# Folding two pieces of an expert's first weights at a time, over four PSUM banks

## Chip, cores and metric

The kernel runs on one core of a Trainium2 chip. The metric is the device time of one execution in microseconds (us).

## What is computed

Three stages in float32: attention through 32 packed tokens a head, four experts whose outputs are weighted, and a two-layer MLP. The sizes: batch 4, 8 heads, 576 tokens, head size 64 (2304 rows of 512 in all); the experts go from 512 to 1024 and back, the last layer from 512 to 2048 and back.

```
p_packed = sm_attn(p, k, v)               # 32 rows a head
x = sm_attn(q, p_packed, p_packed)        # reshaped to 2304 x 512
for e in range(4):
    h = max(x @ w1[e], 0)
    out += p[:, e:e+1] * (h @ w2[e])
g = s * max(out @ w_in, 0)**2 + b
y = g @ w_out
```

## The kernel before

Every product is done in three matmuls of float32r halves (low x high, high x high, high x low); a tile called `hi` is the rounded value and `lo` the rest.

The attention's last product and the experts' first are joined: instead of `(a @ p_packed) @ w1` the kernel multiplies `p_packed @ w1` first, once for each batch, and calls that the fold. Its result `w1p` (128 packed rows of a head group by 512 columns, hi and lo) is then the stationary operand of `m1` (line 726), which makes `h`; ScalarE and VectorE evict `h` as `hh` and `hl` (lines 747 and 749), and `m2` (line 772) adds their products with `w2` into `acc`.

The experts run through 256 steps: expert `e`, batch `bi`, half `hf` of the tokens, block `f` of 128 columns, 16 steps a batch. `m1` runs two steps ahead of `m2`. `m2` holds two or three of four PSUM banks (`acc0` to `acc3`, taken in turn); `h` has two, and the tag `m` has two.

Expert 0's folds are done in place for each batch. For experts 1 to 3 the fold is done for all batches at once, in pieces named by expert, column half `n` (columns 0 to 511 or 512 to 1023), head group `gi` and `x`:

- `load_w1b` (line 519) loads `w1r` for one (`n`, `gi`), 512 KB;
- `split_w1b` (529) makes its hi and lo for one `x`, on ScalarE and VectorE;
- `fold_heads` (541) does six matmuls into the two `m` banks: for `z` 0 and 1 in turn the upper or lower 64 rows of the array, three products each (tile `pp`, line 546), then four evictions to `w1o` (ScalarE line 552, VectorE line 553);
- `store_heads` (558) stores two `w1o` of 512 KB to `w1p_dram` (line 561, issued by SP);
- `load_w1p` (567) later loads a batch's `w1p`, four pieces of 128 KB (line 573, SP), which wait for the stores that they read.

An expert has 8 such pieces, three experts 24. `w1r` and `w1o` share seven buffers (`take` and `give`, first given, first taken) with `last_weights` (line 617), which converts the last layer's float64 weights (`wi0raw` and so on) along the way.

Work is put into a table by step (`at`); at each step what stands there is issued in the order in which it was put in, then `m1`, then `m2`. Each engine and SP's queue work strictly in that order. `load_w2` (line 590) loads one block `w2r` of 256 KB into one of five buffers, which `split_w2` (598) frees: ScalarE makes `w2h` (603), GpSimd `w2l` (606).

Of the kernel before, what the change touches and what calls it, by code (L numbers as in the profile page):

```python
# [8 lines left out]
F32 = mybir.dt.float32  # L9
F32R = mybir.dt.float32r  # L10
U32 = mybir.dt.uint32
AF = mybir.ActivationFunctionType
ALU = mybir.AluOpType
# [6 lines left out]
def attention_experts_mlp_kernel(  # L20
# [25 lines left out]
    nc = tc.nc  # L46
# [5 lines left out]
    P = 128  # L52
    G = 2
    HT = S // 2
    HF = F // 2
    NF = F // P
    KB = DM // P
# [20 lines left out]
    ps_m = stack_a.enter_context(tc.tile_pool(name="ps_m", bufs=2, space=PSUM))  # L78
# [3 lines left out]
    def f32(ap):  # L82
        return ap.bitcast(F32)
# [115 lines left out]
    def flip_p():  # L199
        t = bank("pflip")  # L200
        for i in range((B - FINE) * G):
            nc.tensor.transpose(t[:64, i * P : (i + 1) * P], p_in[:, FINE * G + i], ident)
        t = t[:64].rearrange("d (i x c) -> d i x c", x=2, c=64)
        for x in range(2):
            nc.scalar.activation(pflip[half(x)], t[:, :, x], AF.Copy)
# [3 lines left out]
    def bank(name, tag="m"):  # L209
        pool = {"m": ps_m, "h": ps_h}.get(tag, ps_acc)  # L210
        return pool.tile([P, 512], F32, tag=tag, name=name)

    def half(x):
        return slice(64 * x, 64 * x + 64)

    def at_s1(bi, h, tags="mm"):
        ps = stt["s1", bi, h] = [bank(f"s1_{bi}{h}{c}", tags[c]) for c in range(2)]
        if bi >= FINE:
            for g in range(G):
                for z in range(2):  # L220
                    for x in range(2):
                        r = 64 * g + 32 * z
                        i = (bi - FINE) * G + g
                        nc.tensor.matmul(  # L224
                            ps[x][r : r + 32, :HT],
                            lhsT=pflip[half(x), i, 32 * z : 32 * z + 32],
                            rhs=kqT["k", bi, g][half(x), z, h * HT : (h + 1) * HT],
                            start=True,
                            stop=True,
                        )  # L230
            return
        for e in range(2):
            for g in range(G):
                for c in range(2):
                    x = kqT["k", bi, g][half(c), e]
                    t = ps[c][half(g), :HT]
                    if bi == 0:
                        x = x.rearrange("a (r j) -> a r j", j=NJ)[:, :, blocks((h,))[0]]
                        t = t.rearrange("a (r j) -> a r j", r=32)
                    else:  # L240
                        x = x[:, h * HT : (h + 1) * HT]
                    nc.tensor.matmul(  # L242
                        t, lhsT=pbd[bi][half(c), g, e, :], rhs=x, start=(e == 0), stop=(e == 1)
                    )
# [39 lines left out]
    def at_a1t(bi, gi, tags="mm"):  # L284
        a1, _, _ = stt["a1", bi, gi]
        a1c = a1[:, : VC * P].rearrange("a (r c) -> a c r", c=VC)
        at = att.tile([P, VC + 1, P], F32, tag="a1t", bufs=2, name=f"a1t_{bi}{gi}")
        t = bank(f"tr_{bi}{gi}0", tags[0])
        for c in range(VC):
            nc.tensor.transpose(t[:, c * P : (c + 1) * P], a1c[:, c, :], ident)  # L290
        nc.scalar.activation(
            at[:, :VC, :].rearrange("r c a -> r (c a)"), t[:, : VC * P], AF.Copy
        )
        t = bank(f"tr_{bi}{gi}1", tags[1])
        nc.tensor.transpose(t[:VR, :P], a1[:, VC * P :], ident)
        nc.scalar.activation(at[:VR, VC, :], t[:VR, :P], AF.Copy)
        stt["a1t", bi, gi] = at
# [147 lines left out]
    def take(shape, dt, name):  # L445
        tag = free4.pop(0)
        return tag, wf.tile(shape, dt, tag=tag, bufs=1, name=name)
# [44 lines left out]
    w1s = {}  # L492
# [6 lines left out]
    pth = {}  # L499
# [38 lines left out]
        if x == 1:  # L538
            give(w1q[e, n, gi])

    def fold_heads(e, n, gi, x):
        ps = [ps_m.tile([P, 512], F32, tag="m", name=f"pp1_{e}{n}{gi}{x}{z}") for z in range(2)]
        for i, (a, w) in enumerate(((1, 0), (0, 0), (0, 1))):
            for z in range(2):
                r = slice(64 * z, 64 * z + 64)
                nc.tensor.matmul(  # L546
                    ps[z], lhsT=pth[a][r, gi, x, :], rhs=w1s[e, n, gi][w][r, x, :],
                    start=(i == 0), stop=(i == 2),
                )
        for z in range(2):  # L550
            q, t = take([P, 2, HF], F32R, f"w1o_{e}{n}{gi}{x}{z}")
            nc.scalar.activation(t[:, 0], ps[z], AF.Copy)  # L552
            nc.vector.tensor_tensor(out=t[:, 1], in0=ps[z], in1=f32(t[:, 0]), op=ALU.subtract)  # L553
            w1o[e, n, gi, x, z] = q, t

    w1o = {}

# [161 lines left out]
    hh, rest, acc, xt, x2 = {}, {}, {}, {}, {}  # L719
# [116 lines left out]
    xs, gg, o_acc, o_sb, sx, yy = {}, {}, {}, {}, {}, {}  # L836
# [157 lines left out]
    with tc.manual_schedule():  # L994
# [8 lines left out]
        for gi in range(G):  # L1003
# [3 lines left out]
            out=p_rows[:NB], in_=probs.rearrange("(j a) e -> j (a e)", a=P)  # L1007
# [123 lines left out]
        SB = 2 * NF  # L1131

        def at(step, fn, *args):
            weave.setdefault(step, []).append((fn, args))
# [5 lines left out]
        def mid(step):  # L1140
            return "mid", step
# [23 lines left out]
        for n in range(1, B):  # L1165
            s0 = (n - 1) * SB + (4 if n == 1 else 0)
# [34 lines left out]
        for e in range(E):  # L1201
            for bi in range(B):
                s0 = (e * B + bi) * SB
                ne, nb = (e, bi + 1) if bi + 1 < B else (e + 1, 0)
                if ne == E:
                    continue
                for n in range(2 if ne == 0 else 0):
                    for fn in (fold_w1, fold_hi, fold_lo):
                        step = s0 + 11 + 4 * n
                        at(mid(step) if nb == 1 and n == 0 else step, fn, nb, n)  # L1210
                for c in range(4):
                    n, gi = divmod(c, 2)
                    if ne:
                        d = c + 4 * (ne == 1 and nb == 1) if nb else ((6, 7, 13, 14) if ne > 1 else (8, 8, 12, 12))[c]
                        at(s0 + d, load_w1p, ne, nb, n, gi)
                    if bi != B - 1:
                        continue
                    for x in range(2):
                        k = 2 * c + x
                        if ne == 1:  # L1220
                            d = s0 + 2 + k
                        elif n:
                            d = s0 + 2 * k - 7
                        elif ne == 2:
                            d = s0 - SB + 8 + 2 * k
                        else:
                            d = s0 - 2 * SB + NF + 2 * k
                        if x == 0:
                            at(max(d - 4, s0) if ne == 1 else d - 4, load_w1b, ne, n, gi)
                        at(d, split_w1b, ne, n, gi, x)  # L1230
                        at(d + 1, fold_heads, ne, n, gi, x)
                        at(d + (2 if ne == 1 else 3), store_heads, ne, n, gi, x)
                if bi == B - 1:
                    for f in range(NF):
                        at(s0 + (f // 2 if f < 5 else 5 + f) if ne == 1 else s0 + 6 + f, load_w2, ne, f)
                        at(s0 + 9 + f, split_w2, ne, f)
# [17 lines left out]
        s0 = (E * B - 2) * SB  # L1254
# [142 lines left out]
```

## Time and profile before

| what | value |
|---|---|
| median of 3 runs | 1078.56 us |
| lowest and highest | 1077.34 and 1079.09 us |
| span of the profiled execution, first to last instruction | 1076.6 us |
| time of runs beyond that span (1078.56 - 1076.6) | 2.0 us |
| busy: TensorE matmuls, weight loads | 1065.9 us, 906.2 us |
| busy: VectorE, ScalarE, GpSimd | 657.2, 442.5, 181.3 us |
| TensorE's granted clock | 1.0 of full speed throughout |

The profile is of one execution, whose own time is known by its span; the 2.0 us are the difference to the runs' median. Busy time of TensorE counts matmuls whose ends are modelled and which overlap, so starts are the better measure there: the distance from one start to the next is what the engine spent. Idle time of the other engines costs nothing as long as TensorE doesn't wait for them.

### The profile page before, as it was taken

Reading aid. Unit: us, or ns where it says so; the run is one execution under the profiler, and the core shown is the slowest. Engines: PE = TensorE matmul, PEld = TensorE weight load, DVE = VectorE, ACT = ScalarE, POOL = GpSimd, SP = SyncE. Lnnn points to the kernel's source line nnn. Section 1 sums busy time; section 2 is a strip of 40 time slices with the busy share of each in tenths; the row PEclk is TensorE's granted clock in tenths of the full one; section 3 lists DMA queues with packets and bytes.
Section 4 is the critical chain, followed back from the end, with each engine's and each line's share of the span. In section 5 each row is a group of like instructions: output and inputs, shape, how many; then the busy total and the mean of one; then the engine's idle time right before and its main releaser. Section 6 shows DMA issues by size and latency. Waiting matters only on the chain.

```text
span 1076.6 us, 16978 instructions
## 1 busy us (share of the span) xinstructions
PE 1065.9 (99%) x6215; PEld 906.2 (84%) x6215; DVE 657.2 (61%) x1291; ACT 442.5 (41%) x991; POOL 181.3 (17%) x201
## 2 busy tenths in 40 slices
PE   8999999999999999999999999999999999999998
PEld 5777778788887888888888888988888888888887
DVE  7885765645365445565465645699745766775554
ACT  3533333543234343433434765766532332343111
POOL 0620312131010131010221123023101120210000
PEclk9999999999999999999999999999999999999999
DMA  9853330976555775574766242256856555665532
GB/s 267 199 108 77 50 109 19 331 217 187 143 163 213 252 188 137 187 235 161 249 171 174 68 128 118 98 193 227 330 178 216 190 200 181 209 209 183 186 108 88
DMA packets 107037, 187.01 MB, mean 174 GB/s; under 512 B 49465, under 2 KB 64057, under 8 KB 106955
## 3 DMA queue, kind: packets, MB, share of 16 engines
q1 hardware_dynamic: 106107, 184.82, 55.0%
q10 hardware_dynamic: 848, 1.11, 0.4%
q8 instruction: 49, 0.80, 0.3%
q14 instruction: 33, 0.27, 0.1%
HBM read 131.11 MB, written 54.79 MB: 173 GB/s over the span
## 4 chain that ended last, share of the span: by engine, by line
PE 93%; DVE 2%; DMA 2%; SPq 1%; issue 1%; ACT 0%; POOL 0%; DVEq 0%; ACTq 0%
PE acc L772 36%; PE h L726 19%; PE o L972 19%; PE h L936 16%; PE pp L546 2%; DMA v<-in_v_dram 1%; DMA raw<-in_moe_w_dram 1%; PE pv L308 1%; PE pw L470 0%; PE s L375 0%; PE tr L290 0%; SPq L148 0%; DVE xs L879 0%; PE s L224 0%; PE s L242 0%
## 5 line engine op out<-in xcount | busy, mean ns | idle before, releaser
L726 PEld LDWEIGHTS h<-a,w1p 128*128 128x128 f32 x1536 | 227.5, 188 | 35.5 <-issue 9.0
L726 PE MATMUL h<-a,w1p 128*128 128x320 f32 (+1 forms) x1536 | 250.7, 299 | 0.5 <-DVE hl L749 0.3
L749 DVE SCALAR_TENSOR_TENSOR hl<-h,hh 128x256 fp32r<-128x256 f32 x256 | 107.4, 420 | 203.4 <-ACT rest L747 102.2
L972 PE MATMUL o<-wo,gg 128*128 128x512 f32 x864 | 224.8, 394 | 0.0
L936 PE MATMUL h<-xs,wop 128*128 128x384 f32 x1008 | 203.8, 338 | 1.5 <-DVE yy L956 1.5
L772 PE MATMUL acc<-w2l,hh 128*128 128x512 f32 x512 | 201.9, 394 | 0.2 <-POOL w2l L606 0.2
L772 PE MATMUL acc<-w2h,hh 128*128 128x512 f32 x512 | 201.4, 393 | 0.0
L772 PE MATMUL acc<-w2h,hl 128*128 128x512 f32 x512 | 200.4, 391 | 0.0
L936 PEld LDWEIGHTS h<-xs,wop 128*128 128x128 f32 x1008 | 180.5, 188 | 16.2 <-DVE yy L956 1.8
L972 PEld LDWEIGHTS o<-wo,gg 128*128 128x128 f32 x864 | 160.2, 188 | 24.8 <-DVE gg L902 0.4
L747 ACT ACTIVATE hh<-h 128x256 fp32r<-128x256 f32 x256 | 98.3, 384 | 191.6 <-PE h L726 187.8
L772 PEld LDWEIGHTS acc<-w2h,hl 128*128 128x128 f32 x512 | 96.2, 188 | 21.9
L772 PEld LDWEIGHTS acc<-w2l,hh 128*128 128x128 f32 x512 | 96.3, 188 | 15.8 <-issue 0.4
L772 PEld LDWEIGHTS acc<-w2h,hh 128*128 128x128 f32 x512 | 96.3, 188 | 13.2
L888 ACT ACTIVATE yy<-yy 128x768 f32<-128x768 f32 x48 | 40.2, 838 | 110.0 <-DVE yy L956 110.0
L956 DVE TENSOR_TENSOR yy<-h,uv 128x384 f32<-128x384 f32 x96 | 51.0, 552 | 49.5 <-PE h L936 49.2
L898 ACT ACTIVATE gg<-yy,b_sb 128x768 fp32r<-128x768 f32 x48 | 44.8, 934 | 33.7 <-DVE yy L891 32.4
L553 DVE TENSOR_TENSOR w1o<-pp,w1o 128x512 fp32r<-128x512 f32 x48 | 30.9, 686 | 43.5 <-ACT w1o L552 43.5
L606 POOL TENSOR_TENSOR w2l<-w2r,w2h 128x512 fp32r<-128x512 f32 x24 | 31.3, 1304 | 138.5 <-ACT w2h L603 137.7
L902 DVE SCALAR_TENSOR_TENSOR gg<-yy,b_sb,gg 128x768 fp32r<-128x768 f32 x48 | 52.7, 1098 | 0.4 <-ACT gg L898 0.4
L956 DVE TENSOR_TENSOR uv<-h,uv 128x384 f32<-128x384 f32 x48 | 26.4, 554 | 38.7 <-PE h L936 38.7
L891 DVE SCALAR_TENSOR_TENSOR yy<-yy,s_sb 128x768 f32<-128x768 f32 x48 | 49.7, 1035 | 0.0
(392 smaller groups left out, 1080.7 us busy)
## 6 DMA issues: line engine op xcount, KB each, us to landing
xs<-xs_dram SPq DMA_DIRECT2D x63, 768.0 KB, 4.3
w1p_dram<-w1o SPq DMA_DIRECT2D x48, 512.0 KB, 3.7
w1p<-w1p_dram SPq DMA_DIRECT2D x192, 128.0 KB, 4.3
xs_dram<-xs SPq DMA_DIRECT2D x21, 768.0 KB, 3.3
w1r<-in_moe_w_dram SPq DMA_DIRECT2D x12, 512.0 KB, 4.3
w2r<-in_moe_w_dram SPq DMA_DIRECT2D x24, 256.0 KB, 4.3
out_dram<-o_sb SPq DMA_DIRECT2D x17, 256.0 KB, 2.0
v<-in_v_dram SPq DMA_DIRECT2D x8, 512.0 KB, 6.0
```

The lines of the kernel that those rows point to most:

```text
L606: nc.gpsimd.tensor_tensor(out=lo, in0=raw_t.pop((e, f)), in1=f32(hi), op=ALU.subtract)
L726: nc.tensor.matmul(t[:, : width(bi, hf)], lhsT=w1p_block(e, bi, f, gi, w), rhs=a2[bi][:, x, gi, part(bi, hf)], start=(n == 0), stop=(n == ...
L747: nc.scalar.activation(hi, src, AF.Relu)
L749: nc.vector.scalar_tensor_tensor(out=lo, in0=src, scalar=0.0, in1=f32(hi), op0=ALU.max, op1=ALU.subtract)
L772: nc.tensor.matmul(acc[j], lhsT=x, rhs=w, start=(f == 0 and n == 0), stop=(g == NF - 1 and n == 2),)
L888: nc.scalar.activation(y, y, AF.Relu)
L891: nc.vector.scalar_tensor_tensor(out=y, in0=y, scalar=s_sb, in1=y, op0=ALU.mult, op1=ALU.mult)
L898: nc.scalar.activation(t[:, 0], y, AF.Identity, bias=b_sb)
L902: nc.vector.scalar_tensor_tensor(out=t[:, 1], in0=y, scalar=b_sb, in1=f32(t[:, 0]), op0=ALU.add, op1=ALU.subtract)
L936: nc.tensor.matmul(ps, lhsT=w[:, a, col], rhs=x[:, z, m, :], start=(n == 0), stop=(n == 3 * HK - 1),)
L956: nc.vector.tensor_tensor(out=dst, in0=ps, in1=src, op=ALU.add)
L972: nc.tensor.matmul(o_acc[i], lhsT=lhsT, rhs=w, start=(f == 0 and n == 0), stop=(f == FG - 1 and n == 2),)
```

## The change

`fold_heads` takes a list of `x`. The first piece still goes to the two `m` banks; a second one goes to two banks of `acc` that `m2` doesn't hold at that time (`spare`). Its six matmuls follow the first piece's directly; the eight evictions follow in turn. Expert 1's first column half is folded in single pieces at the steps of before. All other pieces are folded in pairs, and the table of steps is rewritten for them: the second column half of each expert at steps 10 and 12 of its last batch ahead (before: 7 to 10 for expert 1; 2, 4, 6, 8 for experts 2 and 3), its stores at 12 and 14, its `w1p` loads for batch 0 at 13 and 15 (before: 12 and 12, or 13 and 14). The first use of them stays at step 18, two steps into the new expert.

```diff
+    def spare(i, name):
+        return bank(name, f"acc{-(acc['n'] + i) % KB}")
...
+    def fold_heads(e, n, gi, xs):
+        ps = {}
+        for x in xs:
             for z in range(2):
-                r = slice(64 * z, 64 * z + 64)
-                nc.tensor.matmul(
-                    ps[z], lhsT=pth[a][r, gi, x, :], rhs=w1s[e, n, gi][w][r, x, :],
-                    start=(i == 0), stop=(i == 2),
+                name = f"pp1_{e}{n}{gi}{x}{z}"
+                if x == xs[0]:
+                    ps[x, z] = ps_m.tile([P, 512], F32, tag="m", name=name)
+                else:
+                    ps[x, z] = spare(1 + z, name)
+        for x in xs:
+            for i, (a, w) in enumerate(((1, 0), (0, 0), (0, 1))):
+                for z in range(2):
+                    r = slice(64 * z, 64 * z + 64)
+                    nc.tensor.matmul(
+                        ps[x, z], lhsT=pth[a][r, gi, x, :], rhs=w1s[e, n, gi][w][r, x, :],
+                        start=(i == 0), stop=(i == 2),
+                    )
...
-                        d = c + 4 * (ne == 1 and nb == 1) if nb else ((6, 7, 13, 14) if ne > 1 else (8, 8, 12, 12))[c]
+                        d = c + 4 * (ne == 1 and nb == 1) if nb else ((6, 7, 13, 15) if ne > 1 else (8, 8, 13, 15))[c]
                         at(s0 + d, load_w1p, ne, nb, n, gi)
...
+                    if ne == 1 and n == 0:
+                        for x in range(2):
+                            d = s0 + 2 + 2 * c + x
+                            if x == 0:
+                                at(max(d - 4, s0), load_w1b, ne, n, gi)
+                            at(d, split_w1b, ne, n, gi, x)
+                            at(d + 1, fold_heads, ne, n, gi, (x,))
+                            at(d + 2, store_heads, ne, n, gi, x)
+                        continue
+                    d = s0 + 10 + 2 * gi if n else {
+                        2: s0 - SB + 10, 3: s0 - 2 * SB + 10
+                    }[ne] + 3 * gi
+                    at(d - 7, load_w1b, ne, n, gi)
                     for x in range(2):
...
+                        at(d - 3 + x + (n and gi), split_w1b, ne, n, gi, x)
+                        at(d + 2, store_heads, ne, n, gi, x)
+                    at(d, fold_heads, ne, n, gi, (0, 1))
```

On TensorE, the last two pieces of expert 1 (`pp1_11100` to `pp1_11111`; the digits are expert, `n`, `gi`, `x`, `z`). Before, from the end of the first piece to the start of the second:

```order
L546 MATMUL pp1_11100_2740<-w1l_111_2715,pth0_2400 128x512
L546 MATMUL pp1_11101_2741<-w1l_111_2715,pth0_2400 128x512
L726 MATMUL h_0313_2760<-a2_3_2227,w1p_0300_2252 128x256 x3
L726 MATMUL h_0313_2760<-a2_3_2227,w1p_0301_2254 128x256 x3
L772 MATMUL acc_016_2730<-w2l_01_430,hh_0311_2674 128x512
L772 MATMUL acc_016_2730<-w2h_01_429,hh_0311_2674 128x512
L772 MATMUL acc_016_2730<-w2h_01_429,hl_0311_2675 128x512
L772 MATMUL acc_017_2734<-w2l_01_430,hh_0311_2674 128x512
L772 MATMUL acc_017_2734<-w2h_01_429,hh_0311_2674 128x512
L772 MATMUL acc_017_2734<-w2h_01_429,hl_0311_2675 128x512
L546 MATMUL pp1_11110_2781<-w1h_111_2714,pth1_2401 128x512
L546 MATMUL pp1_11111_2782<-w1h_111_2714,pth1_2401 128x512
```

and now, the same two pieces whole, between the `acc` matmuls of one step and the next `h`:

```order
L557 MATMUL pp1_11100_2811<-w1h_111_2755,pth1_2401 128x512
L557 MATMUL pp1_11101_2812<-w1h_111_2755,pth1_2401 128x512
L557 MATMUL pp1_11100_2811<-w1h_111_2755,pth0_2400 128x512
L557 MATMUL pp1_11101_2812<-w1h_111_2755,pth0_2400 128x512
L557 MATMUL pp1_11100_2811<-w1l_111_2756,pth0_2400 128x512
L557 MATMUL pp1_11101_2812<-w1l_111_2756,pth0_2400 128x512
L557 MATMUL pp1_11110_2813<-w1h_111_2755,pth1_2401 128x512
L557 MATMUL pp1_11111_2814<-w1h_111_2755,pth1_2401 128x512
L557 MATMUL pp1_11110_2813<-w1h_111_2755,pth0_2400 128x512
L557 MATMUL pp1_11111_2814<-w1h_111_2755,pth0_2400 128x512
L557 MATMUL pp1_11110_2813<-w1l_111_2756,pth0_2400 128x512
L557 MATMUL pp1_11111_2814<-w1l_111_2756,pth0_2400 128x512
```

A step's `h` and `acc` no longer stand between the two pieces, and the last piece stands two steps later (ahead of `h_0316` instead of `h_0314`).

On SP's queue, the end of expert 1's second column half (`w1o` the stores, `w1p_101` the loads of expert 1, batch 0, second half; `w2r` the blocks of `w2`). Before:

```order
L561 DMA w1p_dram1_90<-w1o_11100_2748 128x1024
L561 DMA w1p_dram1_90<-w1o_11101_2751 128x1024
L595 DMA w2r_15_2799<-in_moe_w2_dram 128x512
L561 DMA w1p_dram1_90<-w1o_11110_2789 128x1024
L561 DMA w1p_dram1_90<-w1o_11111_2792 128x1024
L595 DMA w2r_16_2824<-in_moe_w2_dram 128x512
L573 DMA w1p_1010_2843<-w1p_dram1_90 32x1024 x4
L573 DMA w1p_1011_2848<-w1p_dram1_90 32x1024 x4
L595 DMA w2r_17_2857<-in_moe_w2_dram 128x512
L627 DMA wi0raw_2880<-in_moe2_w_in_dram 128x4x256
L627 DMA wi1raw_2946<-in_moe2_w_in_dram 128x4x256
```

and now:

```order
L609 DMA w2r_16_2788<-in_moe_w2_dram 128x512
L575 DMA w1p_dram1_90<-w1o_11000_2743 128x1024
L575 DMA w1p_dram1_90<-w1o_11001_2746 128x1024
L575 DMA w1p_dram1_90<-w1o_11010_2749 128x1024
L575 DMA w1p_dram1_90<-w1o_11011_2752 128x1024
L609 DMA w2r_17_2843<-in_moe_w2_dram 128x512
L587 DMA w1p_1010_2862<-w1p_dram1_90 32x1024 x4
L641 DMA wi0raw_2871<-in_moe2_w_in_dram 128x4x256
L575 DMA w1p_dram1_90<-w1o_11100_2827 128x1024
L575 DMA w1p_dram1_90<-w1o_11101_2830 128x1024
L575 DMA w1p_dram1_90<-w1o_11110_2833 128x1024
L575 DMA w1p_dram1_90<-w1o_11111_2836 128x1024
```

The next row now is `w1p_1011`, the loads that read the last four stores. `w2r_16` moved ahead of the first pair's stores, and the loads `w1p_1010`, which read those, moved ahead of the second pair's stores. In experts 2 and 3 the `w2r` of block 5 stands ahead of the first pair's stores, that of block 6 behind them, that of block 7 in the place of `wi0raw`; the rest is in the same order.

## Rows read from the trace of the kernel before

**Rows 1.** Busy time, share of the span, instructions (page, part 1).

```profile
PE 1065.9 (99%) x6215; PEld 906.2 (84%) x6215; DVE 657.2 (61%) x1291; ACT 442.5 (41%) x991; POOL 181.3 (17%) x201
```

**Rows 2.** The chain that ended last, by engine and by line (page, part 4).

```profile
PE 93%; DVE 2%; DMA 2%; SPq 1%; issue 1%; ACT 0%; POOL 0%; DVEq 0%; ACTq 0%
PE acc L772 36%; PE h L726 19%; PE o L972 19%; PE h L936 16%; PE pp L546 2%; DMA v<-in_v_dram 1%; DMA raw<-in_moe_w_dram 1%; PE pv L308 1%; PE pw L470 0%; PE s L375 0%; PE tr L290 0%; SPq L148 0%; DVE xs L879 0%; PE s L224 0%; PE s L242 0%
```

**Rows 3.** Timeline of plain steps: start us, us, engine, line, operation.

```profile
262.14 1.04 PE L726 MATMUL h<-a,w1p 128*128 128x320 f32 x6
...
265.08 1.04 PE L726 MATMUL h<-a,w1p 128*128 128x320 f32 x6
```

**Rows 4.** Timeline of TensorE around single folds of expert 2, in narrow windows.

```profile
344.55 0.39 PE L772 MATMUL acc<-w2h,hl 128*128 128x512 f32 x1
344.86 0.50 PE L546 MATMUL pp<-w1h,pth 64*128 64x512 f32 x2
...
345.20 0.39 PE L546 MATMUL pp<-w1h,pth 64*128 64x512 f32 x2
345.43 0.40 PE L546 MATMUL pp<-w1l,pth 64*128 64x512 f32 x2
345.76 1.15 PE L726 MATMUL h<-a,w1p 128*128 128x320 f32 x6
...
348.81 1.04 PE L726 MATMUL h<-a,w1p 128*128 128x320 f32 x6
...
352.74 1.15 PE L726 MATMUL h<-a,w1p 128*128 128x320 f32 x6
```

**Rows 5.** Timeline of TensorE from expert 1's last fold to its second half.

```profile
210.32 0.73 PE L546 MATMUL pp<-w1h,pth 64*128 64x512 f32 x4
...
211.22 0.98 PE L726 MATMUL h<-a,w1p 128*128 128x256 f32 x6
213.40 0.88 PE L726 MATMUL h<-a,w1p 128*128 128x256 f32 x6
...
228.13 0.88 PE L726 MATMUL h<-a,w1p 128*128 128x256 f32 x6
```

**Rows 6.** Timelines of ScalarE and VectorE around that fold.

```profile
209.09 0.63 ACT L536 ACTIVATE w1h<-w1r 128x512 fp32r<-128x512 f32 x1
209.61 0.63 ACT L603 ACTIVATE w2h<-w2r 128x512 fp32r<-128x512 f32 x1
...
211.32 1.09 ACT L552 ACTIVATE w1o<-pp 128x512 fp32r<-128x512 f32 x2 [0.80 <-PE pp L546]
212.29 0.64 ACT L603 ACTIVATE w2h<-w2r 128x512 fp32r<-128x512 f32 x1
...
210.90 0.74 DVE L790 TENSOR_SCALAR xt<-acc,p_tok 128x512 f32<-128x512 f32 x1
```

**Rows 7.** Timeline of SP's queue there, one DMA issue a row.

```profile
211.81 0.33 SPq L595 DMA_DIRECT2D w2r<-in_moe_w_dram  x1
212.67 0.48 SPq L561 DMA_DIRECT2D w1p_dram<-w1o  x1
213.27 1.40 SPq L561 DMA_DIRECT2D w1p_dram<-w1o  x1
```

**Rows 8.** Single issues at 187.01, (187.61), 194.50, 551.21: KB, us to landing.

```profile
w1p_dram<-w1o SPq DMA_DIRECT2D x1, 512.0 KB, 5.3
...
187.61 0.44 SPq L521 DMA_DIRECT2D w1r<-in_moe_w_dram  x1
...
w1p_dram<-w1o SPq DMA_DIRECT2D x1, 512.0 KB, 2.8
...
w1p<-w1p_dram SPq DMA_DIRECT2D x1, 128.0 KB, 2.8
```

**Rows 9.** Stretches: us, PE, PEld, DVE, ACT, POOL busy, granted clock, DMA share, GB/s.

```profile
208.00:214.00 6.00, 6.00 (x38) 4.79 (x37) 5.03 (x9) 4.68 (x10) 2.46 (x2) 1.00 1.03 416
...
380.00:386.00 6.00, 6.00 (x35) 5.21 (x34) 2.59 (x5) 2.42 (x5) 3.88 (x3) 1.00 1.04 234
```

More of the change, by code (lines that the diff above doesn't have):

```diff
@@ L539, in split_w1b @@
             give(w1q[e, n, gi])
-    def fold_heads(e, n, gi, x):
-        ps = [ps_m.tile([P, 512], F32, tag="m", name=f"pp1_{e}{n}{gi}{x}{z}") for z in range(2)]
-        for i, (a, w) in enumerate(((1, 0), (0, 0), (0, 1))):
+    def fold_heads(e, n, gi, xs):
+        ps = {}
+        for x in xs:
             for z in range(2):
-                r = slice(64 * z, 64 * z + 64)
-                nc.tensor.matmul(
-                    ps[z], lhsT=pth[a][r, gi, x, :], rhs=w1s[e, n, gi][w][r, x, :],
-                    start=(i == 0), stop=(i == 2),
-                )
[L550 to L554, printed above, removed]
+                name = f"pp1_{e}{n}{gi}{x}{z}"
[11 more added lines that the diff above has]
+                    )
+        for x in xs:
+            for z in range(2):
+                q, t = take([P, 2, HF], F32R, f"w1o_{e}{n}{gi}{x}{z}")
+                nc.scalar.activation(t[:, 0], ps[x, z], AF.Copy)
+                nc.vector.tensor_tensor(
+                    out=t[:, 1], in0=ps[x, z], in1=f32(t[:, 0]), op=ALU.subtract
+                )
+                w1o[e, n, gi, x, z] = q, t
     w1o = {}
@@ L1217, in attention_experts_mlp_kernel @@
                         continue
-                    for x in range(2):
[L1219 to L1232, printed above, removed]
+                    if ne == 1 and n == 0:
[11 more added lines that the diff above has]
+                    at(d - 7, load_w1b, ne, n, gi)
+                    for x in range(2):
+                        at(d - 3 + x + (n and gi), split_w1b, ne, n, gi, x)
+                        at(d + 2, store_heads, ne, n, gi, x)
+                    at(d, fold_heads, ne, n, gi, (0, 1))
                 if bi == B - 1:
```

## Prediction, before the changed kernel was run

> **What bounds the kernel now.** I read the busy shares first, then the chain that ended last, then TensorE's own timeline. TensorE is busy 99% of the 1076.6 us span [rows 1], and the chain gives it 93%, of which 2% are the folds' matmuls, `pp` [rows 2]. The reader is to see that nothing else can give time back unless TensorE issues faster, and that anything that makes TensorE wait is paid in full. The profiled execution's span is 1076.6; the median of the runs, 1078.56, stands 2.0 above it (start and end outside the span), and I carry these 2.0 over. A measurement of this kernel tells 0.2%, or 2.2 us, from no change.
>
> **What a single fold costs.** Two plain steps of expert 2's stretch start 265.08 - 262.14 = 2.94 us apart [rows 3]. Around one fold the step ahead of it takes 352.74 - 348.81 = 3.93 and the step behind such a fold 348.81 - 345.76 = 3.05 [rows 4]. So one fold costs 3.93 + 3.05 - 2 x 2.94 = 1.10 us. Inside it the three pairs of row halves start at 344.86, 345.20 and 345.43, and the next `h` at 345.76 [rows 4]: slots of 0.34, 0.23 and 0.33. Only the middle one is the pace of the work; the rest is entering and leaving.
>
> **What pairing gives.** Of 24 folds, 4 stay single (expert 1's first half) and 20 become 10 pairs. A second piece behind the first adds three slots at the middle pace, 0.69, so a pair costs 1.79 instead of 2.20: 0.41 saved, 4.1 us over 10 pairs. If every added slot cost as the first does (0.34, 1.02 in all), the saving would be 0.18 each, 1.8 us. I take 4.1, since the first slot's extra belongs to the entry. The spare banks could make the second piece wait: the last sum of the half before leaves on VectorE at 210.90 for 0.74 us [rows 6], 1.32 after a fold that began at 210.32 [rows 5], and the second piece begins at 0.69. That bounds it at 0.63 for each expert's first late pair; I take nothing, because the older fold's VectorE work that now stands ahead of that sum is gone.
>
> **What moves, and what it collides with.** The second half of each expert's pieces (columns 512 and up) is now folded at steps 10 and 12 of the last sixteen before that expert; before, the last was at step 10 (expert 1) or 8. Its rows must be stored, and loaded again as `w1p`, before the `h` of step 18 that first uses them. I count from the first late pair's start, 0.
> - When they are needed. The `h` behind a fold starts at 0.90 (211.22 - 210.32), the next 2.18 later, and a plain step is 2.10 (213.40 to 228.13 is seven of them) [rows 5]. A fold begins 0.31 after the last `acc` matmul instead of 0.23 [rows 4]. So: `h` at 0.90 + 0.69 = 1.59, next 3.77, second pair 2.10 + 0.08 later at 5.95, `h` 7.54, 9.72, then five steps: 20.2. Half its products on, at 20.6, the second pair's rows are wanted.
> - When stores can go. A fold that began at 210.32 has its first store issued at 212.67, the next at 213.27 [rows 5, 7]. So a pair's four go at 2.35, 2.95, 3.55 and 4.15, the second pair's from 8.3 to 10.1.
> - What a store takes. One on an idle queue lands 2.8 us after issue [rows 8]. At 416 GB/s [rows 9] its 512 KB need 1.26, so 1.5 is fixed; four in a row land 1.5 + 4 x 1.26 = 6.5 after the first issue. An issue holds SP up to 0.5 [rows 7].
> - Experts 2 and 3. The first four land at 8.9, 9.5 with the 256 KB `w2r` issued among them. SP stands there: the loads of the first pair's rows wait for these landings, and the second pair's stores are queued behind. Load and `w2r` issue until 9.9, stores from 10.4 to 11.7, landing at 16.9, or 17.6 with that other data. The last two loads go out 0.5 apart to 18.1; an undisturbed one takes 2.8 [rows 8]: 20.9, against 20.6. Were the stores as slow as the 234 GB/s at which loads of `w1p` were seen [rows 9], 2.24 each, it would be 24.2. I take 0.9 of waiting for each, near the first, since stores are what moves; bounds 0 and 3.6.
> - Expert 1. Here `w2r_16` stands ahead of the first stores, and it waits for the GpSimd split of `w2` block 1, whose ScalarE part is behind the pair's four evictions. Evictions begin 1.0 after the fold and two take 0.97 of ScalarE (211.32 to 212.29), a copy 0.52 (209.09 to 209.61); from the ScalarE part (209.61) to the `w2r` that waits for its block (211.81) it is 2.2 [rows 5 to 7]. So 1.0 + 1.94 + 0.52 + 2.2 = 5.7. Stores go from 6.1 and land at 12.6, or 13.2 with the `w2r` data; `wi0raw` (512 KB) goes at 13.7, the second stores from 14.2. They land at 20.7 if nothing interferes and 22.9 with `wi0raw` at 234 GB/s (2.2); the last load, 0.5 + 2.8 on, at 24.0 to 26.2. I take 25.8, a wait of 5.2, because `wi0raw` is sure to be in the queue ahead; bounds 3.4 and 7, the upper one with the same loss on the stores as above, halved.
>
> A rule bears on the order of landings. A store with a 512 KB load issued 0.6 behind it took 5.3 us instead of 2.8 [rows 8]: later transfers do slow earlier ones, and the sum counts that. The Trainium skill, page DMA: Bandwidth & Descriptors, section "Two DMAs through the same engine are not ordered", says descriptors of one queue start in order but are pipelined. Read strictly, `w2r` would not delay stores ahead of it and experts 2 and 3 would wait about 0.6 less each; the row speaks against the strict reading.
>
> **The sum.** -4.1 + 5.2 + 2 x 0.9 = +2.9 us: span 1079.5, time 1078.6 + 2.9 = **1081.5**. The splits and evictions that move are costed at nothing, since ScalarE and VectorE hold 0 and 2% of the chain [rows 2] and TensorE's two steps of lead cover them. That cover goes if an eviction waits for a buffer's store: the second pair reuses the first's buffers, whose stores land at up to 9.5 while ScalarE wants them by 5.95 + 1.0 + 1.5 = 8.4; `hh` behind it would then be late next. In the sum it costs nothing extra, since the later wait for `w1p` swallows it.
>
> **Rivals.**
> 1. *The rows come in time* (the other side). If SP sends the second stores at once and the landings overlap fully, the load lands by 20.6 everywhere: 1078.6 - 4.1 = 1074.5. For it: in experts 2 and 3 my gap is only 0.3 before mixed traffic. Against: in expert 1 even the lower bound is 3.4 late. It decides where the last load lands before 20.6 after the pair. Chance 0.14.
> 2. *Only expert 1 waits.* -4.1 + 5.2 = +1.1: 1079.7, no change to a measurement. For it: the bound 0 for the others. Chance 0.18.
> 3. *The wait costs the clock too.* All stretches here show a granted clock of 1.00 [rows 9], the 2.4 GHz level, and no row shows a fall. If 5 us of waiting drops it to 1.2 GHz for one or two steps of 2.1 us of work, each such step costs itself once more: 2.1 to 4.2 on top of 1081.5, 1083.6 to 1085.7. The Trainium skill, page TensorE: Matmul & The Clock Gate, section "Part 1: The HAM clock gate", says that an idle array falls to the lower level and gets back only through sustained activity; no run here shows it yet. Chance 0.18.
>
> That the change doesn't do what it says is excluded by the order of instructions: twelve fold matmuls stand in one block.
>
> **How the numbers follow.** The forecast (all three experts wait) has 0.50, its own range 1079 to 1084; some 0.14 of it lies below 1080.7. Faster by over 0.2% (below 1076.4) is rival 1: 0.14. Same is rival 2 and that part: 0.32. Slower is the rest with rival 3: 0.54. The range reaches from rival 1 to rival 3, 1074.5 to 1085.5, leaving out half of the first and about half of the last.
>
> **What would show it.** Right: `pp` blocks of 12 matmuls with a total of about 1.79; TensorE waiting for `w1p<-w1p_dram` three times, at the first `h` of each later expert's second half, longest at expert 1; SP waiting behind `w2r_16` there. Wrong: no such wait, or a pair costing 2.0 or more; a granted clock below 1.00 behind expert 1's wait would be rival 3.

## The result, and the profile after

The changed kernel takes 1089.45 us (median of 4 runs, 1088.09 to 1091.57) beside 1078.74 for the kernel before on the same chip: a ratio of 1.0107, 95% interval 1.0094 to 1.0119 (the two medians alone give 1.0099), slower by 10.7 us. The forecast was 1081.5, in a range from 1074.5 to 1085.5: the direction is right, the size is not. The profiled execution has a span of 1087.9 us, 11.3 more than before.

The page of the changed kernel, busy times and the chain that ended last, answers to [rows 1, 2]:

```profile
PE 1065.8 (98%) x6215; PEld 910.2 (84%) x6215; DVE 663.0 (61%) x1291; ACT 439.6 (40%) x991; POOL 182.4 (17%) x201
...
PE 90%; DMA 5%; DVE 3%; ACT 1%; issue 1%; SPq 1%; POOL 0%; DVEq 0%; ACTq 0%
PE acc L786 34%; PE o L986 18%; PE h L740 18%; PE h L950 15%; DMA w1p_dram<-w1o 2%; PE pp L557 2%; DMA raw<-in_moe_w_dram 1%; DMA w1p<-w1p_dram 1%; PE pv L311 1%; DMA k<-in_k_dram 1%; PE pw L473 0%; PE tr L293 0%; PE s L378 0%; PE s L245 0%
```

The work is the same, TensorE is busy for 1065.8 us as before; the chain now runs 5% through DMAs (2% before), and two of them are new in it: the stores of `w1o` and the loads of `w1p`. The list of waits of TensorE (total, times, longest) names the place. This wait isn't in the list of the kernel before:

```profile
PE h L740 <- DMA w1p<-w1p_dram: 10.0, 3, 6.8
```

**The pairs are nearly as cheap as forecast.** TensorE's timeline at expert 1's two late pairs (start us, us, engine, line, operation) answers to [rows 5]:

```profile
207.37 0.73 PE L557 MATMUL pp<-w1h,pth 64*128 64x512 f32 x4
207.94 0.40 PE L557 MATMUL pp<-w1l,pth 64*128 64x512 f32 x2
208.18 0.62 PE L557 MATMUL pp<-w1h,pth 64*128 64x512 f32 x4
208.64 0.40 PE L557 MATMUL pp<-w1l,pth 64*128 64x512 f32 x2
208.97 0.98 PE L740 MATMUL h<-a,w1p 128*128 128x256 f32 x6
...
213.37 0.73 PE L557 MATMUL pp<-w1h,pth 64*128 64x512 f32 x4
```

Twelve matmuls stand in one block; `h` follows 208.97 - 207.37 = 1.60 us behind its start (1.59 forecast) and the second pair starts 6.00 behind the first (5.95). Over the stretches without a wait the steps gain as they should: from the third step of expert 1's second half to the first late use at expert 2, with four pairs, 395.17 - 241.53 = 153.64 us against 155.16 for the same steps before, and the next such stretch 155.68 against 157.27. That is 1.52 and 1.59, or 0.38 and 0.40 a pair, where 0.41 was expected. Expert 1's two pairs give less, 0.44 together up to the wait; one step behind them, at 217.17, is 0.23 longer than before.

**The three waits cost 14.4.** TensorE's timeline at the first `h` of each later expert's second half, with the wait in brackets:

```profile
228.03 0.52 PE L740 MATMUL h<-a,w1p 128*128 128x256 f32 x3
235.38 0.98 PE L740 MATMUL h<-a,w1p 128*128 128x256 f32 x3 [6.83 <-DMA w1p<-w1p_dram]
236.16 0.63 PE L786 MATMUL acc<-w2l,hh 128*128 128x512 f32 x1
236.58 0.63 PE L786 MATMUL acc<-w2h,hh 128*128 128x512 f32 x1
...
238.72 1.48 PE L740 MATMUL h<-a,w1p 128*128 128x256 f32 x6
...
241.53 0.87 PE L740 MATMUL h<-a,w1p 128*128 128x256 f32 x6
...
396.85 0.59 PE L740 MATMUL h<-a,w1p 128*128 128x256 f32 x3 [1.16 <-DMA w1p<-w1p_dram]
...
556.84 0.59 PE L740 MATMUL h<-a,w1p 128*128 128x256 f32 x3 [1.97 <-DMA w1p<-w1p_dram]
```

At expert 1 two steps take 241.53 - 228.03 = 13.50 us; two plain steps [rows 5] take 4.21, so 9.3 are lost, of which 6.83 are the wait. At expert 2 one step takes 3.50 instead of 2.11 (1.4 lost, 1.16 waited), at expert 3 two steps take 7.97 instead of 4.22 (3.75 lost, 1.97 waited). The sum is 14.4: 10.0 of waiting and 4.4 behind it (2.5, 0.2 and 1.8 by expert). With the 3.55 that steps without a wait give back (0.44, 1.52 and 1.59), 10.9 remain, the 10.7 of the medians.

What stands behind the waits is TensorE's pace. After the wait two `acc` matmuls start 236.58 - 236.16 = 0.42 us apart; before and elsewhere it is 0.23. The stretches around (us; PE, PEld, DVE, ACT, POOL busy; granted clock; DMA share; GB/s) show why, where every stretch of before had 1.00 [rows 9]:

```profile
230.00:235.00 5.00, 0.00 (x0) 0.00 (x0) 0.00 (x0) 0.00 (x0) 0.00 (x0) 0.85 0.58 171
235.00:240.00 5.00, 4.62 (x16) 4.07 (x17) 1.79 (x4) 1.10 (x2) 0.00 (x0) 0.50 0.56 188
240.00:245.00 5.00, 5.00 (x28) 4.38 (x28) 1.78 (x4) 1.87 (x4) 1.29 (x1) 0.97 0.21 61
395.00:400.00 5.00, 3.84 (x23) 3.25 (x22) 1.94 (x5) 2.19 (x4) 0.00 (x0) 1.00 0.96 244
...
555.00:560.00 5.00, 3.16 (x12) 2.71 (x13) 1.42 (x3) 0.47 (x2) 0.89 (x1) 0.77 0.97 241
560.00:565.00 5.00, 5.00 (x28) 4.41 (x27) 2.02 (x6) 2.00 (x4) 0.41 (x1) 0.89 1.03 282
```

While TensorE stands idle at expert 1 the granted clock falls; it is 0.50 of full speed (the 1.2 GHz level) from 235 to 240 us, as TensorE takes up work again, and back at 1.00 within the stretch behind. At expert 3 it also falls, after a wait of 1.97; at expert 2, after 1.16, it doesn't.

**Why the rows come so late at expert 1.** SP's timeline, one DMA issue a row (start us, how long it held SP), read in narrow windows; to compare with [rows 7]:

```profile
213.27 0.35 SPq L609 DMA_DIRECT2D w2r<-in_moe_w_dram  x1
213.72 0.38 SPq L575 DMA_DIRECT2D w1p_dram<-w1o  x1
...
215.73 1.19 SPq L575 DMA_DIRECT2D w1p_dram<-w1o  x1
...
221.70 0.42 SPq L641 DMA_DIRECT2D wi0raw<-in_moe_w_in_dram  x1
222.16 0.50 SPq L575 DMA_DIRECT2D w1p_dram<-w1o  x1
...
224.45 1.60 SPq L575 DMA_DIRECT2D w1p_dram<-w1o  x1
...
232.71 0.30 SPq L587 DMA_DIRECT2D w1p<-w1p_dram  x1
```

The issues of 215.73, 222.16 and 224.45 in the list of DMAs (KB each, us from issue to landing):

```profile
w1p_dram<-w1o SPq DMA_DIRECT2D x1, 512.0 KB, 5.6
...
w1p_dram<-w1o SPq DMA_DIRECT2D x1, 512.0 KB, 6.0
...
w1p_dram<-w1o SPq DMA_DIRECT2D x1, 512.0 KB, 7.5
```

The pair starts at 207.37. SP stands before `w2r_16` until +5.9; the first pair's four stores go from +6.35, the last lands at 215.73 + 5.6, +14.0; `wi0raw` goes at +14.3, the second stores from +14.8 and the last of them lands at 224.45 + 7.5 = 231.95, +24.6. The last load goes out at +25.3 and `h` starts at +28.0. The rows were wanted at 235.38 - 6.83, +21.2.

Three stretches of the changed kernel in the same columns as above, to compare with [rows 9]:

```profile
215.00:220.00 5.00, 4.92 (x30) 4.06 (x29) 3.19 (x6) 3.34 (x8) 1.20 (x1) 1.00 1.02 412
222.00:225.00 3.00, 3.00 (x20) 2.64 (x19) 1.08 (x2) 1.83 (x4) 2.15 (x3) 1.00 1.00 219
225.00:229.00 4.00, 3.55 (x20) 2.90 (x18) 1.84 (x4) 1.22 (x3) 1.02 (x1) 1.00 1.04 415
```

The DMA engines are busy throughout. In the first and the last stretch, with stores in the queue, they move 412 and 415 GB/s. From 222 to 225, when the loads of the first pair's `w1p` land (the last at 224.7) and `wi0raw` is in the queue, they move 219.

### The profile page after: what moved, and what is told of

Same layout as the page of the kernel before. It is cut to its first block, busy times and chain, and to the rows that moved or that the text cites. A ratio compares the mean times of both kernels' runs of the same rounds, so it can differ in the third digit from the quotient of the medians.

```text
span 1087.9 us, 16975 instructions
## 1 busy us (share of the span) xinstructions
PE 1065.8 (98%) x6215; PEld 910.2 (84%) x6215; DVE 663.0 (61%) x1291; ACT 439.6 (40%) x991; POOL 182.4 (17%) x201
## 2 busy tenths in 40 slices
DMA packets 107037, 187.01 MB, mean 172 GB/s; under 512 B 49465, under 2 KB 64057, under 8 KB 106955
## 4 chain that ended last, share of the span: by engine, by line
PE 90%; DMA 5%; DVE 3%; ACT 1%; issue 1%; SPq 1%; POOL 0%; DVEq 0%; ACTq 0%
PE acc L786 34%; PE o L986 18%; PE h L740 18%; PE h L950 15%; DMA w1p_dram<-w1o 2%; PE pp L557 2%; DMA raw<-in_moe_w_dram 1%; DMA w1p<-w1p_dram 1%; PE pv L311 1%; DMA k<-in_k_dram 1%; PE pw L473 0%; PE tr L293 0%; PE s L378 0%; PE s L245 0%; SPq L148 0%
## 5 line engine op out<-in xcount | busy, mean ns | idle before, releaser
L740 PEld LDWEIGHTS h<-a,w1p 128*128 128x128 f32 x1536 | 229.8, 190 | 44.0 <-issue 20.2
L986 PEld LDWEIGHTS o<-wo,gg 128*128 128x128 f32 x864 | 160.1, 188 | 24.9 <-DVE gg L916 0.5
L916 DVE SCALAR_TENSOR_TENSOR gg<-yy,b_sb,gg 128x768 fp32r<-128x768 f32 x48 | 52.0, 1084 | 0.2 <-ACT gg L912 0.2
L1002 DVE TENSOR_TENSOR o_sb<-o,o_sb 128x512 f32<-128x512 f32 (+1 forms) x55 | 36.9, 675 | 16.7 <-PE o L986 16.7
```

The source lines that it names most:

```text
L740: nc.tensor.matmul(t[:, : width(bi, hf)], lhsT=w1p_block(e, bi, f, gi, w), rhs=a2[bi][:, x, gi, part(bi, hf)], start=(n == 0), stop=(n == ...
L916: nc.vector.scalar_tensor_tensor(out=t[:, 1], in0=y, scalar=b_sb, in1=f32(t[:, 0]), op0=ALU.add, op1=ALU.subtract)
L986: nc.tensor.matmul(o_acc[i], lhsT=lhsT, rhs=w, start=(f == 0 and n == 0), stop=(f == FG - 1 and n == 2),)
L1002: nc.vector.tensor_tensor(out=dst[:, c], in0=acc[:, c], in1=dst[:, c], op=ALU.add)
```

## Experiments

Each kernel was timed beside the kernel before on one chip; the chip is not the same for all of them, so a loss is best read against its own before. Theory L says that the late rows cost the time; P, that the pairs themselves do; the other letters are given with their run.

| kernel | median us | ratio to before, 95% interval |
|---|---|---|
| the change | 1089.45 | 1.0107 (1.0094 to 1.0119) |
| `warm`: fill matmuls ahead of the waits | 1087.71 | 1.0081 (1.0067 to 1.0095) |
| `late_single`: late steps, no pairs | 1086.11 | 1.0075 (1.0060 to 1.0090) |
| `late_wi`: `wi0raw` behind the loads | 1084.70 | 1.0062 (1.0045 to 1.0078) |
| `order1`: `w2r_16` behind the stores | 1082.84 | 1.0044 (1.0030 to 1.0058) |
| `order2`: that, and `wi0raw` earlier | 1082.99 | 1.0039 (1.0027 to 1.0052) |
| `early`: expert 1 as before, the pairs of 2, 3 earlier | 1082.00 | 1.0032 (1.0019 to 1.0044) |
| `one_back`: expert 1 as before | 1081.05 | 1.0021 (1.0010 to 1.0033) |
| `spread`: eight pairs, none late in twos | 1076.90 | 0.9987 (0.9976 to 0.9998) |
| `spread2`: that, splits a step earlier | 1076.91 | 0.9980 (0.9971 to 0.9989) |

The median of before was 1078.74 beside the change, 1078.81 beside `early`, `one_back`, `warm` and `order2`, 1078.29 beside `spread`, `late_single` and `order1`, 1078.65 beside `late_wi` and `spread2`. In the diffs `...` stands for changed or unchanged lines that are left out.

### Is it the placement or the pairs?

`late_single` keeps the change's late steps and folds nothing in pairs:

```diff
-                        at(d + 2, store_heads, ne, n, gi, x)
-                    at(d, fold_heads, ne, n, gi, (0, 1))
+                        at(d + 1 + x, store_heads, ne, n, gi, x)
+                        at(d - 1 + x, fold_heads, ne, n, gi, (x,))
```

> The change's late steps, but every pair is undone into two single pieces in consecutive steps, so nothing is paired and only the placement is left. L (late rows): the waits of the change stay, somewhat shorter because the first stores can go a step earlier (expert 1 by 4 to 7 us with the clock, experts 2 and 3 by 0 to 4 each), and the 4.1 us that pairing gives are gone: 1084 to 1092. P (the pairs themselves): as before, 1078 to 1080.

1086.11, 7.8 above before, with not one pair in it. TensorE waits 4.51 at expert 1 (its first store goes 4.5 behind the start of the first late piece, 209.17 - 204.71, where the change has 6.35) and 0.44 at expert 3. So P falls, and the loss belongs to the steps at which the pieces are folded.

`one_back` is the other half: expert 1's second half goes back to single pieces at the old steps, the eight pairs of experts 2 and 3 stay as changed.

```diff
...
-                    if ne == 1 and n == 0:
+                    if ne == 1:
```

> Only expert 1 goes back to single pieces and to its old steps; experts 2 and 3 stay as in the change. Theory L: expert 1's wait (6.8 us in the trace) and the low clock behind it go, two pairs' gain with them; what is left against the kernel before is -3.3 for eight pairs, +1.4 at expert 2 and +3.8 at expert 3: about 1080.6. Rival P (the pairs as such cost): the loss goes with the number of pairs, 8 of 10, so about 1087.

1081.05: about 8.4 of the 10.7 are expert 1's. Its two waits that are left, at experts 2 and 3, last 0.89 and 1.62, and the granted clock stays at 1.00 behind both. From the first `h` of expert 0 to the last `acc` of expert 3 its trace is 0.9 us shorter than before's (675.4 against 676.3), but 0.8 of that is one step of expert 0 (at 47.8 us), which the edit doesn't touch; from there on the eight pairs' gain and the two waits cancel. The median is 2.2 above before. The executions differ in the clock: four of the ten have a mean granted clock of 0.996 to 0.998 and took 1081.8 to 1083.0 us; the other six, with the profiled one at 1078.28, have 0.999 or 1.000 and took 1078.0 to 1081.8.

### What makes expert 1's rows late

`order1` moves one DMA issue: `w2r_16` behind the first pair's stores.

```diff
-                        at(s0 + (f // 2 if f < 5 else 5 + f) if ne == 1 else s0 + 6 + f, load_w2, ne, f)
+                        at(s0 + (f // 2 if f < 5 else max(5 + f, 6 + f if f == 6 else 0)) if ne == 1 else s0 + 6 + f, load_w2, ne, f)
```

> The change, with one DMA issue moved on SP's queue: w2r_16 goes behind the first late pair's four stores at expert 1 instead of ahead of them; wi0raw stays. L with SP's order as the cause: the first stores go about 3.4 us earlier, so expert 1's wait falls from 6.8 to about 3.4 and less of the clock is lost, 1084 to 1086. B (the stores and loads take their own time however they are queued): wait within 1 of 6.8, 1088 to 1090.

`order2` has the same line and issues `wi0raw` four steps earlier as well (`if n == 0 and d == -4: step -= 4`).

> The change as it is, but for expert 1 two transfers are moved on SP's queue: w2r_16 behind the first pair's stores instead of ahead of them, and wi0raw four steps earlier, out of the way of the second pair's stores. Theory L with SP's order as the reason for expert 1's long wait: its stores go at once, 4 us earlier, and the queue has 0.5 MB less in it when it matters; the wait falls from 6.8 us to 0 to 2.5, its low clock goes with it, about 1081 to 1083. Rival B (the transfers' own time is the reason, 16 stores at their rate): the wait stays above 5 us, about 1088.

1082.84 and 1082.99. TensorE's timeline at expert 1's wait in `order1`:

```profile
231.73 0.98 PE L740 MATMUL h<-a,w1p 128*128 128x256 f32 x3 [3.84 <-DMA w1p<-w1p_dram]
```

In `order2` it is 2.18. Beside their own kernel before, the loss is 4.6 and 4.2 us instead of 10.7, so B falls, and `order1` gains more than L gave it (1084 to 1086). Not all of these 6 us is shown to be the issue's place on SP's queue: in the traces expert 1's steps lose 5.5 instead of 9.3, 3.8 less, and another 2.1 is gone at expert 3, where the edit changes nothing and the clock stayed at 1.00 this time. Moving `wi0raw` forward as well shortens the wait further and brings nothing that the runs' spread (1080.87 to 1084.94) would show.

`late_wi` asks the other way round. `w2r_16` stays ahead of the stores; `wi0raw` and the start of its conversion go two steps later, behind the loads of `w1p`.

```diff
                 step = calm[3 * n + d] if 3 * n + d >= 0 else calm[0] + 3 * n + d
+                if n == 0:
+                    step += 2
```

> The change, with wi0raw (512 KB) taken off SP's queue ahead of expert 1's second stores and put behind the last two w1p loads; its conversion starts two steps later. w2r_16 stays where the change has it. M (the other data in the queue slowed the second stores, 9.8 us from the first issue to the last landing): they go about 0.5 us earlier and land within 6.5 to 7.3 us of their first issue, so expert 1's wait falls from 6.8 to between 3 and 4.2, and with less lost clock the time is 1083.5 to 1086.5. S (the stores need that long by themselves): landing takes 9 us or more, wait 6 to 6.8, 1087.5 to 1089.5.

1084.70. The first and the last of the second stores on SP's timeline:

```profile
220.43 0.42 SPq L575 DMA_DIRECT2D w1p_dram<-w1o  x1
...
222.32 1.17 SPq L575 DMA_DIRECT2D w1p_dram<-w1o  x1
```

The last one in the list of DMAs, and TensorE's wait:

```profile
w1p_dram<-w1o SPq DMA_DIRECT2D x1, 512.0 KB, 5.8
```

```profile
231.41 0.98 PE L740 MATMUL h<-a,w1p 128*128 128x256 f32 x3 [4.25 <-DMA w1p<-w1p_dram]
```

From the first issue to the last landing it is 222.32 + 5.8 - 220.43 = 7.7 us; with `wi0raw` in front it was 231.95 - 222.16 = 9.8. So `wi0raw` cost the stores 2.1, and M holds. 7.7 is what four stores take there without it: a little above the 7.3 that M allowed, as is the wait (4.25 for 4.2). `order1` and `order2` give a second, smaller price: 9.7 for the second stores with `wi0raw` just ahead, 8.3 with it four steps earlier, 1.4. The Trainium skill, page DMA: Bandwidth & Descriptors, section "Two DMAs through the same engine are not ordered", says that descriptors of one queue start in order and are pipelined. In the change's trace all landings listed for SP's queue from 207 to 234 us come in the order of issue, which agrees as far as it goes. That the stores pay for `wi0raw` because it starts first isn't shown; data issued behind a store slows it too [rows 8].

### Is the clock part of the price?

`warm` is the change with matmuls that nobody reads ahead of the three waiting `h` (32, 6 and 10 of 128x512, by expert), so that TensorE isn't idle while the rows come:

```diff
+        fill = {1: 32, 2: 6, 3: 10}.get(e, 0) if (bi, hf, f) == (0, 0, NF // 2) else 0
+        if fill:
+            busy = ps_m.tile([P, 512], F32, tag="m", name=f"busy{e}")
+            for _ in range(fill):
+                nc.tensor.matmul(
+                    busy, lhsT=w1p_block(e, bi, 0, 0, 0), rhs=a2[bi][:, 0, 0, :512],
+                    start=True, stop=True,
+                )
```

> The change as it is, and ahead of the h that waits, TensorE is given matmuls that nobody reads (32 for expert 1, 6 for expert 2, 10 for expert 3, 512 columns each, about 6.9, 1.3 and 2.2 us), so that it is busy while the rows come. Theory L with the clock as part of the price: the granted clock stays at 1.00, the wait for the rows is as long, and the 2.3 us behind expert 1's wait and 1.8 behind expert 3's are saved: about 1085.5. Rival D (what follows the wait is not the clock, but evictions and transfers that are late too): no change, 1089.5, or up to 1090 where the matmuls outlast the wait.

1087.71. The stretches of TensorE's wait and behind it, in `warm`:

```profile
230.00:235.00 5.00, 5.00 (x23) 4.04 (x22) 0.00 (x0) 0.03 (x1) 0.00 (x0) 1.00 0.69 244
235.00:240.00 5.00, 5.00 (x29) 4.32 (x28) 1.79 (x4) 1.26 (x3) 0.00 (x0) 1.00 0.71 223
```

The clock stays at 1.00 though the rows come hardly earlier (the last load goes out at 233.56, 24.9 behind the first late pair; 25.3 in the change), and the three places lose 7.5, 1.5 and 2.3 us, 11.3 instead of 14.4. That is nearly all the fill's own time:

```profile
229.29 7.63 PE L740 MATMUL busy<-a,w1p 128*128 128x512 f32 x32
236.76 0.88 PE L748 MATMUL h<-a,w1p 128*128 128x256 f32 x6
```

The `h` follows it without a wait, 236.76 - 229.29 = 7.47 us behind its start, 0.233 for each of the 32; 48 make 11.2. So the fill was up to 1.2 longer than the 10.0 of waiting in the change, and the 3.1 saved in the traces are a lower bound there for what the clock cost, which the change's trace puts at up to 4.4. The medians show 1.7, less than the 4 that L put in. D, that keeping TensorE busy changes nothing, doesn't fit the trace. The executions bear the clock out: its mean is 0.999 to 1.000 in all four of `warm`, 0.990 to 0.997 in the four of the change. The time lies between the two expectations, and its interval overlaps that of the change slightly. So that the clock is part of the price is shown; how much of it stays open, between 1.7 and 4.4. The Trainium skill, page TensorE: Matmul & The Clock Gate, section "Part 1: The HAM clock gate", says that activity holds the higher level and idleness loses it. The traces agree: 0.50 after the idle wait, 1.00 with the fill.

### Earlier instead of later

`early` leaves expert 1 as before and folds expert 2's pairs and the late pairs of expert 3 a whole batch earlier:

```diff
...
-                    d = s0 + 10 + 2 * gi if n else {
-                        2: s0 - SB + 10, 3: s0 - 2 * SB + 10
-                    }[ne] + 3 * gi
+                    d = s0 - (2 - n) * SB + 10 + 3 * gi
...
```

> Expert 1 is folded in single pieces at its old steps; experts 2 and 3 keep all eight pairs, but both halves are folded one batch earlier, so that their rows are stored long before the first use. Theory L (late rows): all that was lost were TensorE's waits for w1p and what followed them; without them eight pairs give 8 x 0.41 = 3.3 us, so about 1075.4, with no wait for w1p at all. Rival P (the pairs themselves cost: eight evictions in one go, sums kept out of two acc banks): the pairs are all there, so it stays above the kernel before, 1080 or more. Rival N (pairing gives nothing): 1078.7.

1082.0, a clear miss. By its number alone it would fit P (1080 or more); the trace shows another cause. No `h` waits for `w1p` any more, but one waits for something else. Views of `early` around 495 us: TensorE, ScalarE, SP, and SP's longest wait ahead of these stores:

```profile
500.51 1.94 PE L740 MATMUL h<-a,w1p 128*128 128x320 f32 x6 [3.90 <-DVE rest L763]
```

```profile
495.98 0.60 ACT L564 ACTIVATE w1o<-pp 128x512 fp32r<-128x512 f32 x1 [1.98 <-DMA w1p_dram<-w1o]
497.30 0.60 ACT L564 ACTIVATE w1o<-pp 128x512 fp32r<-128x512 f32 x1 [0.72 <-DMA w1p_dram<-w1o]
498.58 0.60 ACT L564 ACTIVATE w1o<-pp 128x512 fp32r<-128x512 f32 x1 [0.69 <-DMA w1p_dram<-w1o]
```

```profile
490.02 0.33 SPq L646 DMA_DIRECT2D wo10raw<-in_moe_w_out_dram  x1
492.51 0.33 SPq L676 DMA_DIRECT2D wo_dram<-wo8a  x1
492.88 3.16 SPq L575 DMA_DIRECT2D w1p_dram<-w1o  x4
```

```profile
SPq L646 <- DVE w1l L540: 7.0, 1, 7.0
```

Expert 3's second half now falls among the conversions of the last layer's weights. Two of their issues stand ahead of the first pair's four stores on SP's queue: the load `wo10raw`, which waits 7.0 us until VectorE's split of the second pair's `w1r` is done, and the store `wo8a`, made by GpSimd, which waits 2.1. The second pair's evictions wait for the buffers which those stores free; `hh` and `hl` stand behind the evictions, and `h` for them. It is the stall which the prediction named as "late next" and priced at nothing, at another place. The granted clock is 0.50 in the 5 us from 500 on; the three steps there take 14.23 us instead of 7.46, 6.8 more, which the pairs don't bring in.

`spread` uses what the runs had shown: expert 1's second half is two single pieces at the old steps and one pair at step 10; expert 2 is placed as in `early`; expert 3's second half is two singles at old steps and one pair at step 10. Eight pairs in all.

```diff
...
-                    if ne == 1 and n == 0:
+                    if ne != 2 and (n, gi) in (((0, 0), (0, 1), (1, 0)) if ne == 1 else ((1, 0),)):
...
+                    if ne == 2:
+                        d = s0 - (2 - n) * SB + 10 + 3 * gi
+                    elif n:
+                        d = s0 + 10
...
```

> Eight pairs instead of ten, each placed where its rows have a batch or more, or where only one pair is late: expert 1's second half is two singles at the old steps 8 and 9 and one pair at step 10, expert 2's pairs all stand one batch earlier, expert 3's second half is two singles at steps 3 and 5 and one pair at step 10. L (late rows): no wait of TensorE for w1p<-w1p_dram over 0.5 us, granted clock 1.0, and 8 x 0.41 = 3.3 us saved: 1074.7 to 1076.2. P (the pairs themselves cost time): eight tenths of the loss of the change stays, 1087. N (pairing gives nothing, only waiting mattered): 1078.7 as before.

1076.90, faster than before by 1.4 us instead of 3.3: P, which put it at 1087, falls here too. No `h` of the experts waits for `w1p`, and the granted clock is 1.00 from 26 us to the end of the experts (it was 0.50 ahead of that, at the start, and the profiled execution took 1079.62). At expert 1 the steps are 0.65 longer than before instead of 0.4 shorter, and the timelines of VectorE and TensorE show the wait that the prediction had bounded at 0.63 for a first late pair:

```profile
211.45 1.43 DVE L540 TENSOR_TENSOR w1l<-w1r,w1h 128x512 fp32r<-128x512 f32 x1
...
213.13 0.73 DVE L804 TENSOR_SCALAR xt<-acc,p_tok 128x512 f32<-128x512 f32 x1
...
213.92 0.73 PE L557 MATMUL pp<-w1h,pth 64*128 64x512 f32 x3 [0.41 <-DVE xt L804]
```

The split of the second piece stands on VectorE ahead of the sum that frees the spare bank. `spread2` makes that split one step earlier (`d - 3 + x` for `d - 2 + x`).

> The eight pairs of spread, with the splits ahead of expert 1's late pair one step earlier, so that VectorE's last sum (xt, line 804) no longer stands behind the second piece's split when the pair's spare banks are wanted. L: TensorE's wait of 0.41 us for that sum is gone and with it 0.5 us or so of the steps around: steps 50 to 67 as in the kernel before or 0.3 shorter, 1076.0 to 1076.9. Rival (the pair at this place costs more than elsewhere for another reason): those steps stay 0.65 longer than before, 1076.9 or above.

1076.91 beside 1078.65: 1.7 us faster. The step with the pair takes 3.79 us instead of 4.70, so the wait for `xt` is gone. But these steps end 0.23 longer than before instead of equal, because `h` now waits 0.38 for `w1p` there, and another `h`, at 323.40, waits 0.68 for `rest`, which `spread` didn't. The time is that of `spread` within the intervals: that the wait for `xt` is gone is shown, that it brings time isn't.

## Why the prediction was right or wrong

- **A pair's cost: right.** 0.38 to 0.40 saved a pair at experts 2 and 3 where 0.41 was worked out, 0.22 at expert 1; 3.55 came in by the trace of the 4.1. One slip didn't matter there: by the prediction's own slots the second piece begins 0.34 + 0.23 + 0.23 = 0.80 behind the first, not 0.69 (0.81 in the trace), so the bound for the wait on `xt` was 0.52, not 0.63. In `spread` that wait was 0.41 where nothing was taken for it.
- **Where TensorE waits, and for what: right.** Three times, for `w1p`, at the first `h` of each second half, longest at expert 1, with SP held at `w2r_16` (+5.9 for 5.7). `order1` confirms that this issue matters, `one_back` that most of the loss is expert 1's.
- **The size of the waits: wrong.** The step that failed is "four in a row land 1.5 + 4 x 1.26 = 6.5 after the first issue". Four stores took 7.6 us for the first pair (7.1 forecast, with the `w2r` data) and 7.7 for the second without `wi0raw` (`late_wi`), 1.2 more; at experts 2 and 3 they took 7.6 to 8.2 (7.1 and 7.2 forecast). The rate behind the sum, 416 GB/s, held in the stretches on either side of the one where `w1p` loads landed (412 and 415). What the sum had too little of is the other data in the queue. Beside the first pair's stores went two `w2r`, `w2r_16` and `w2r_17`; it counted one, 0.63. The second stores were issued while the first pair's `w1p` loads were landing, 512 KB which it left out; there the engines moved 219 GB/s, near the 234 of such loads [rows 9]. No run takes these loads away, so that they are the whole reason is argued, not shown. The price of `wi0raw`, 2.2, was near what two comparisons give (2.1 and 1.4). So `h` went on at +28.0 where 25.8 was forecast, the rows were wanted at +21.2 for 20.6, and the wait was 6.83 for 5.2, inside its bounds of 3.4 to 7. At experts 2 and 3 it was 1.16 and 1.97 for 0.9 each, inside 0 to 3.6.
- **Two rows were read too quickly.** "An issue holds SP up to 0.5" passes over the 1.40 in [rows 7]; in the change single stores held SP for up to 1.60 (224.45). The store of 5.3 us in [rows 8] had not only a load 0.6 behind it but also a store 0.6 ahead; the like store at 195.09, with one ahead and nothing behind for 3 us, landed in 3.4. By that comparison the load's share is 1.9, not 2.5. That later transfers slow earlier ones stands.
- **The clock: priced at nothing in the sum, and wrong there.** Rival 3, "The wait costs the clock too", had 0.18 and is what happened. It was given to expert 1 alone, at 2.1 to 4.2; the trace shows about 2.5 there beyond the wait and 1.8 at expert 3, and `warm` gives back 1.7 in the medians and 3.1 in the traces. In the traces of the four other kernels with the same late pairs at expert 3 and no fill (`one_back`, `order1`, `order2`, `late_wi`) the wait was 1.29 to 1.66 and the clock stayed at 1.00 behind it, so that part isn't there in every execution.
- **Why the range failed.** Neither error alone was enough to make 1089.45: waits of 10.0 instead of 7.0 give 1084.5, the clock with the waits as forecast up to 1085.7. Both together, 1081.5 + 3.0 + 4.4, and the 0.5 that the pairs brought less make 1089.4. The range held the one or the other, and ended at 1085.5, below even rival 3's own 1085.7. The clock's price hangs on the waits, so the two should have been added for the upper end.
- **"That cover goes if an eviction waits for a buffer's store": right, and priced too low.** In the change it is nearly swallowed: ScalarE's last eviction of expert 1's second pair waits 1.66 for a store (at 217.60), and a step there is 0.23 longer. In `early` this stall and the low clock behind it were the whole loss.

## What to carry to other kernels

When work is made cheaper by batching it, look at what waits for its result: two pieces in one place come out later than one in each of two places, and every queue that they pass (here SP's, where the issue of one 256 KB load stood ahead) adds its own delay. Batch where there is slack of a whole round trip (store, landing, load) and leave the last pieces single. And price a wait of a busy TensorE above its length: behind the 6.83 us here its clock was half for some microseconds, which cost about 2.5 more.

## What the runs showed that was not expected

The granted clock fell after a wait of only 1.97 us (0.77 in the 5 us around it, steps of 5.08 and 2.89 us for 2.11), while after the 1.16 at expert 2 of the same execution it stayed at 1.00. In `order2` it fell to 0.50 behind a wait of 2.18. At the lower level an `acc` matmul starts every 0.42 us instead of 0.23. And a store on a queue with other traffic costs far more than one alone: 7.5 us to land for the last of four behind `wi0raw`, 5.8 without it, 2.8 for one on an idle queue [rows 8].
